# State sums in other banks, and four small copies on another engine, at a batch's first chunk

## The chip, the cores and the metric

The kernel runs on one core of a Trainium2 chip. The metric is the device time of one execution in microseconds (us), as the median of several runs. Five engines work side by side, each with its own queue of instructions: TensorE (PE in the profile, its weight loads PEld), VectorE (DVE), ScalarE (ACT), GpSimd (POOL) and SyncE (SP), which here only issues DMA transfers. An instruction at the head of a queue that has to wait holds up all that stand behind it on its engine. SBUF is the on-chip memory of 128 partitions; PSUM, in banks of 128 x 512 fp32 values, is where TensorE leaves its products.

## The reference

Two blocks follow each other. The first is a linear attention with decay, in blocks of 64 positions of a sequence of 768, for 4 batches and 8 heads of dimension 64:

```python
for b in range(nb):
    sl = slice(b * block, (b + 1) * block)
    qb, kb, vb = (q[:, :, sl], k[:, :, sl], v[:, :, sl])
    intra = np.einsum('bhic,bhjc->bhij', qb, kb) * Dmask[None]
    intra = np.einsum('bhij,bhjd->bhid', intra, vb)
    inter = np.einsum('bhid,bhde->bhie', qb * lam_pow[None], kv_state)
    out[:, :, sl] = intra + inter
    kb_dec = kb * rev_pow[None]
    kv_state = lam_block[None, :, None, None] * kv_state + np.einsum('bhsd,bhse->bhde', kb_dec, vb)
```

Its output x, as (batch, 768, 512), goes through a mixer: a low-rank product along the sequence that is added to x, and a product with 2048 hidden channels, a maximum with zero, and a product back:

```python
xt = x.transpose(0, 2, 1)
h = xt @ U @ V                       # U: 768 x 32, V: 32 x 768
u = x + h.transpose(0, 2, 1)
ch = np.maximum(u @ w_ch1, 0.0) @ w_ch2
return (u + ch).astype(np.float32)
```

## The kernel before, in words

The kernel treats the sequence in chunks of 128 positions, 6 to a batch, so 24 steps s; c = s mod 6 is the place in the batch and b the batch. A step works all 8 heads. One list, `pieces` (from line 646), written out by hand, gives the order in which the parts of the steps are issued; since each engine takes its instructions in the order of issue, this list sets every queue. The attention stage takes about the first 125 us of the span. Behind it come the two large products of the mixer (`hidden`, lines 830 and 841, and `product`, lines 962 to 966), which TensorE works almost without a gap.

A step's parts, by name and line:

- `prep` (line 361): TensorE turns q and k of the next chunk into two PSUM banks, tag pqk; ScalarE copies them out as qt and kt (line 367).
- `scores` (line 408): k times q into two banks, tag pss; `masked` (line 417): VectorE multiplies them by the decay mask and writes sm.
- `intra` (line 449): sm times v into px. `inter` (line 460): adds q times the state where c > 0; ScalarE then copies px out as x (line 466).
- `state` (line 427): k, scaled by GpSimd (ks, line 381), times v: the state's sums, in one bank. VectorE copies them to SBUF as kv where c = 0 (line 433) or adds the faded old state (line 435; faded is ScalarE's, line 401).
- `scale`: GpSimd's qs (line 392) and ks for the chunk after.
- `mix` (line 561) and `mixed` (line 573), of the chunk seven steps back: the low-rank correction, two matmuls with the high parts of the rows p_hl and two with the low parts, and VectorE's sum with x.
- `turn` (line 624), `split` (lines 638 and 639) and `turned` (line 631): the corrected x turned for the mixer and split into parts.

The rows of the low-rank product of a batch: `low` (line 476) sums them over the batch's six chunks in a bank. ScalarE (line 486) and VectorE (line 518) copy them to SBUF as rows_f, 32 partitions by 512; VectorE masks their high bits into t (line 521). Then `p_hl`, which is part of the tile vp, is filled in three parts that `low_rows` leaves in the list `pps[b]`, and that `next_of_low` takes out one at a time: `spread` copies quarters of t to four groups of 32 partitions (four copies of 32x256, line 529, ScalarE), `low_part` writes the differences rows_f - t into two groups (line 533, GpSimd), and `spread_low` copies these to the two other groups (line 540, ScalarE). The last batch goes another way (lines 496 to 511) that the change doesn't touch. The three parts are issued at the first chunk of the next batch, steps 6, 12 and 18.

The state's sums lie in the banks of tag pm up to step 6, and in those of the scores (pss) from step 7 on.

Of the kernel before, what the change touches and what calls it, by code (L numbers as in the profile page):

```python
# [18 lines left out]
def kernel(  # L19
# [28 lines left out]
    nc = tc.nc  # L48

    B, H, S, D = q.shape  # L50
    HP = H // 2
    NT = S // P
# [51 lines left out]
    def tmp(name):  # L104
        return wconv.tile([P, C], FP32, tag="tmp", bufs=2, name=name)
# [149 lines left out]
    def two_banks(name, tag):  # L255
        return psf.tile([P, 2, N], FP32, tag=tag, name=name)
# [162 lines left out]
    def state(s):  # L419
        c = s % NT  # L420
        if c < NT - 1:
            ks, vr = st[s]["ks"], raw[s, "v"]
            pkv = two_banks("pkv", "pm" if s <= NT else "pss")[:, 0, 0 : HP * D]
            pkv = pkv.rearrange("p (a e) -> p a e", a=HP)
            for a in range(HP):
                for x in range(2):
                    nc.tensor.matmul(  # L427
                        out=pkv[half[x], a, :], lhsT=ks[:, a, x, :], rhs=vr[:, 2 * a + x, :],
                        start=True, stop=True,
                    )  # L430
            kv[s + 1] = att.tile([P, HP, D], FP32, tag="kv", bufs=2, name="kv")
            if c == 0:
                nc.vector.tensor_copy(out=kv[s + 1], in_=pkv)  # L433
            else:
                nc.vector.tensor_tensor(out=kv[s + 1], in0=pkv, in1=st[s]["faded"], op=ALU.add)
# [33 lines left out]
    pps, others = {}, {}  # L469
# [19 lines left out]
    def low_rows(b):  # L489

        pp, t = pps.pop(b), tmp("p_h")[0:R]
        own = [(slice(g * R, (g + 1) * R), slice(g * P, (g + 1) * P)) for g in range(G)]
        if b == B - 1:
            h, h2, l, l2 = (p_hl[g * R : (g + 1) * R] for g in range(G))
            for rows, cols in own:
                nc.vector.tensor_scalar(
                    t[:, cols].bitcast(U32), pp[rows].bitcast(U32), HI, None, ALU.bitwise_and
                )

            def low_part():  # L500
                for rows, cols in own:
                    nc.vector.tensor_tensor(
                        out=l[:, cols], in0=pp[rows], in1=t[:, cols], op=ALU.subtract
                    )

            def spread():
                nc.scalar.copy(h, t)
                nc.scalar.copy(h2, t)

            def spread_low():  # L510
                nc.scalar.copy(l2, l.bitcast(FP32))

            pps[b] = [spread, low_part, spread_low]
            return

        rows_f, pp = pp, others.pop(b)
        for g in range(2, G):
            nc.vector.tensor_copy(
                out=rows_f[:, g * P : (g + 1) * P], in_=pp[g * R : (g + 1) * R]
            )  # L520
        nc.vector.tensor_scalar(t.bitcast(U32), rows_f.bitcast(U32), HI, None, ALU.bitwise_and)
        wide = [slice(x * 2 * P, (x + 1) * 2 * P) for x in range(2)]

        def place(g, low):
            return p_hl[g * R : (g + 1) * R, wide[low]]

        def spread():
            for g in range(G):
                nc.scalar.copy(place(g, 0), t[:, wide[g // 2]])

        def low_part():
            for x in range(2):
                nc.gpsimd.tensor_tensor(
                    out=place(2 * x, 1), in0=rows_f[:, wide[x]], in1=t[:, wide[x]],
                    op=ALU.subtract,
                )

        def spread_low():
            for x in range(2):
                nc.scalar.copy(place(2 * x + 1, 1), place(2 * x, 1).bitcast(FP32))  # L540

        pps[b] = [spread, low_part, spread_low]

    def next_of_low(b):
        pps[b].pop(0)()
# [102 lines left out]
    for s in range(NS):  # L648
        b, c = divmod(s, NT)
        done = s - NT - 1  # L650
        more = s + 1 < NS
        turns = done > 0 and (done - 1) // TG < FG
        mixes = 0 <= done < NS - NT - 1
        rows = c == 0 and b > 0
        step = [("fade", s)] * (c > 0)
        step += [("mix", done)] * mixes + [("turn", done - 1)] * turns
        step += [("split", done - 1)] * turns
        step += [("prep", s + 1)] * more
        step += [("mix", done + 1)] * (not more)
        step += [("next_of_low", b - 1)] * rows + [("next_of_low", b - 1)] * rows  # L660
        step += [("scale", s + 1)] * more
        step += [("mixed", done)] * mixes
        step += [("late", s - 1)] * (1 < s < NT - 1 or s > NT)
        step += [("turned", done - 2)] * (done > 1 and c == 1)
        step += [("mixed", done + 1)] * (not more)
        step += [("next_of_low", b - 1)] * rows
        both = [("intra", s), ("state", s)]
        step += (both if s > NT else both[::-1]) + [("next_v", s), ("inter", s)]
        step += [("late", s)] * (s < 2 or s in (NT - 1, NT))
        step += [("turned", done - 1)] * (done > 0 and c > 0)  # L670
        step += [("scores", s + 1)] * more
        step += [("low", b)] * (more and c == NT - 1)
        step += [("aside", s)] * (0 < s < NT - 2 or s > NT)
        step += [("masked", s + 1)] * more
        step += [("low_rows", b)] * (more and c == NT - 1)
        step += [("aside", s)] * (s in (0, NT - 2, NT - 1, NT))
        step += [("store", done)] * (done >= 0 and done // TG < FG)
        step += [("next_k", s)] * (s > 0)
        pieces += step
    waiting = {name: list(range(NS)) for name in "qkv"}  # L680

    def load_next(name, engine=nc.sync):
# [4 lines left out]
    run = {  # L687
        "prep": prep, "fade": fade, "scores": scores, "masked": masked, "inter": inter,
        "intra": intra, "state": state,
        "low": low, "low_rows": low_rows, "next_of_low": next_of_low, "mix": mix, "turn": turn,  # L690
        "mixed": mixed, "store": store, "next_v": next_v, "split": lambda s: splits.pop(s)(),
        
# [192 lines left out]
    c0, b = NS - NT, B - 1  # L885
# [129 lines left out]
    for i in range(len(steps) - STAG):  # L1015
        g, ft = steps[i]
# [49 lines left out]
```

## Time and profile before

| what | value |
|---|---|
| three runs | 652.66, 656.95, 657.25 us; median 656.95 |
| the profiled execution | 651.98 us, its span 650.1 us |
| granted TensorE clock | 1.000 |
| TensorE busy | 640.0 us, 98% of the span |
| VectorE, ScalarE, GpSimd busy | 441.4, 276.3, 116.6 us |
| the four copies of line 529 | 12 in all, 403 ns each, ScalarE |
| the differences of line 533 | 6 in all, 717 to 1023 ns, GpSimd |
| kv's copy, line 433 | 4 in all, 424 ns, VectorE |

The profile is of one execution. Times in a timeline count from the start of the span. In its lines stand the start, the busy time, the engine, the line of the kernel, the operation, output <- input by the program's names with partitions x elements, and how many of them were merged; in brackets the engine's idle time before, and what ended it. That releaser is inferred: where two ended nearly together, the other may be the one.

### The profile page before, as it was taken

What the parts mean: (1) busy time and instruction counts of PE and PEld (TensorE: products, weight loads), DVE (VectorE), ACT (ScalarE), POOL (GpSimd) and SP (SyncE); (2) the same over time, 40 slices, a digit from 0 to 9 for tenths busy, and PEclk for the clock granted to TensorE, in tenths of its full rate; (3) what the DMA queues carried; (4) which work ended last, traced back from release to release, by engine and by line L of the source; (5) the groups of instructions that cost most, each with busy time, mean ns of one, the idle gap of its engine ahead of it and who ended that gap; (6) DMA issues with size and microseconds to landing.
All of it is one profiled execution on the core that took longest, in us unless ns stands there. A gap on an engine that the chain in (4) does not pass through costs nothing.

```text
span 650.1 us, 13394 instructions
## 1 busy us (share of the span) xinstructions
PE 640.0 (98%) x5242; PEld 538.8 (83%) x5242; DVE 441.4 (68%) x710; ACT 276.3 (43%) x522; POOL 116.6 (18%) x98
## 2 busy tenths in 40 slices
PE   9999999999999999999999999999999999999997
PEld 8888988788888888888888888888888888888886
DVE  6779778658997777777796244685575665755854
ACT  4686876435664444444455221332332322322320
POOL 4476868240000000000000000030030300300300
PEclk9999999999999999999999999999999999999999
DMA  9999994264776656566687999864363363453521
GB/s 227 247 229 254 226 222 126 72 221 164 290 274 212 211 210 212 210 211 211 210 291 265 335 318 385 283 225 148 97 226 98 115 210 98 162 162 98 178 82 65
DMA packets 131776, 131.29 MB, mean 202 GB/s; under 512 B 81346, under 2 KB 89794, under 8 KB 131714
## 3 DMA queue, kind: packets, MB, share of 16 engines
q1 hardware_dynamic: 106592, 124.02, 59.2%
q10 hardware_dynamic: 25122, 6.42, 4.4%
q8 instruction: 41, 0.67, 0.4%
q14 instruction: 21, 0.17, 0.1%
HBM read 80.09 MB, written 50.33 MB: 201 GB/s over the span
## 4 chain that ended last, share of the span: by engine, by line
PE 92%; ACT 3%; DVE 2%; DMA 1%; issue 1%; ACTq 0%; DVEq 0%
PE pz L830 26%; PE pz L962 13%; PE pz L964 13%; PE pd L966 13%; PE pd L841 13%; PE pss L408 3%; PE px L449 3%; PE px L460 2%; PE pqk L361 1%; PE pkv L427 1%; PE pm L561 1%; DMA qraw<-in_q_dram 1%; PE pp L476 1%; DMA kraw<-in_k_dram 1%; PE pm L624 1%
## 5 line engine op out<-in xcount | busy, mean ns | idle before, releaser
L830 PE MATMUL pz<-u_hl,w 128*128 128x512 f32 x768 | 184.5, 390 | 0.0
L830 PEld LDWEIGHTS pz<-u_hl,w 128*128 128x128 f32 x768 | 143.7, 188 | 30.1 <-ACT r L837 0.3
L964 PE MATMUL pz<-w_hl,m 128*128 128x512 f32 x384 | 148.6, 389 | 0.0
L962 PE MATMUL pz<-w_hl,m 128*128 128x512 f32 x384 | 148.2, 389 | 0.0
L966 PE MATMUL pd<-w_d,m 128*128 128x512 f32 x384 | 147.4, 389 | 0.0
L945 ACT ACTIVATE m<-rm 128x512 fp32r<-128x512 f32 x96 | 60.6, 632 | 182.8 <-PE pd L966 125.1
L946 DVE SCALAR_TENSOR_TENSOR m<-rm,m 128x512 fp32r<-128x512 f32 x96 | 71.5, 747 | 95.9 <-ACT m L945 95.8
L991 POOL TENSOR_TENSOR o<-o,u 128x512 f32<-128x512 f32 x20 | 29.8, 1524 | 433.3 <-DVE o L987 433.3
L846 DVE SCALAR_TENSOR_TENSOR r<-pd,r 128x512 f32<-128x512 f32 x96 | 61.7, 684 | 60.3 <-ACT r L837 44.0
L841 PE MATMUL pd<-u_d,w 128*128 128x512 f32 x384 | 95.9, 390 | 0.0
L966 PEld LDWEIGHTS pd<-w_d,m 128*128 128x128 f32 x384 | 72.1, 188 | 15.2 <-DVE m L947 0.3
L964 PEld LDWEIGHTS pz<-w_hl,m 128*128 128x128 f32 x384 | 72.1, 188 | 15.0
L962 PEld LDWEIGHTS pz<-w_hl,m 128*128 128x128 f32 x384 | 72.1, 188 | 14.9
L841 PEld LDWEIGHTS pd<-u_d,w 128*128 128x128 f32 x384 | 71.9, 188 | 14.8
L837 ACT ACTIVATE r<-pz 128x512 f32<-128x512 f32 x96 | 51.8, 590 | 66.6 <-PE pz L830 66.5
L947 DVE SCALAR_TENSOR_TENSOR m<-m 128x512 fp32r<-128x512 f32 x96 | 74.7, 779 | 3.0
L417 DVE TENSOR_TENSOR sm<-pss,mask 128x512 f32<-128x512 f32 x48 | 30.9, 684 | 15.1 <-PE pss L408 14.9
L215 ACT ACTIVATE w<-wf 128x512 fp32r<-128x512 f32 x32 | 20.3, 634 | 34.8 <-DVE wf L197 27.0
L173 ACT ACTIVATE sc<-sc,ends 128x512 f32<-128x512 uint32 x30 | 21.6, 721 | 22.7 <-DVE sc L166 22.7
L408 PE MATMUL pss<-qt,kt 64*128 64x128 f32 x384 | 28.8, 290 | 2.4 <-DVE kv L433 1.2
L449 PE MATMUL px<-vraw,sm 128*64 128x64 f32 x768 | 28.0, 225 | 1.1 <-issue 0.5
L392 POOL TENSOR_TENSOR qs<-qt,powq 128x512 f32<-128x512 f32 x20 | 25.5, 1276 | 18.6 <-ACT qt L367 18.3
(91 smaller groups left out, 626.4 us busy)
## 6 DMA issues: line engine op xcount, KB each, us to landing
r_d<-r SPq DMA_DIRECT2D x96, 256.0 KB, 2.4
rm<-r_d SPq DMA_DIRECT2D x96, 256.0 KB, 2.7
words<-in_moe_w_ch_dram SPq DMA_DIRECT2D x30, 512.0 KB, 4.2
w_d<-w SPq DMA_DIRECT2D x16, 768.0 KB, 3.4
w_hl<-w_d SPq DMA_DIRECT2D x16, 512.0 KB, 6.0
u_d<-x_nat SPq DMA_DIRECT2D x24, 256.0 KB, 3.4
u<-u_d SPq DMA_DIRECT2D x24, 256.0 KB, 4.2
qraw<-in_q_dram SPq DMA_DIRECT2D x23, 256.0 KB, 3.7
```

Of the source, the lines that this page charges most:

```text
L408: nc.tensor.matmul(out=pss[:, x, a, :], lhsT=kt[half[x], a, :], rhs=qt[half[x], a, :], start=True, stop=True,)
L449: nc.tensor.matmul(out=px[half[t], x, a, :], lhsT=sm[:, x, a, half[t]], rhs=vr[:, 2 * a + x, :], start=(a == 0), stop=(alone and a == HP - 1),
L830: nc.tensor.matmul(out=like(acc[g][0], g), lhsT=w[:, n, ct, :], rhs=columns(uhl[g][:, n], g, ct), start=(ct == 0 and n == 0), stop=(ct == ...
L837: nc.scalar.mul(rs[g], acc[g][0], 4096.0 + 1.0)
L841: nc.tensor.matmul(out=like(acc[g][1], g), lhsT=w[:, 2, ct, :], rhs=columns(ud[g], g, ct), start=(ct == 0), stop=(ct == CT - 1),)
L846: nc.vector.scalar_tensor_tensor(rs[g], acc[g][1], 4096.0, rs[g], ALU.mult, ALU.add)
L945: nc.scalar.activation(out=m[:, 0], in_=r, func=AF.Relu, scale=NEAR)
L946: nc.vector.scalar_tensor_tensor(m[:, 1], r, 0.0, hi, ALU.max, ALU.subtract)
L947: nc.vector.scalar_tensor_tensor(m[:, 2], hi, E, low, ALU.mult, ALU.subtract)
L962: nc.tensor.matmul(out=pz, lhsT=m[:, 0, cols], rhs=hl[:, 0], start=first, stop=False)
L964: nc.tensor.matmul(out=pz, lhsT=m[:, 1, cols], rhs=hl[:, 1], start=False, stop=end)
L966: nc.tensor.matmul(out=pd, lhsT=m[:, 2, cols], rhs=dd, start=first, stop=end)
```

## The change

Three things change. At the first chunk of a batch (c = 0) from step 7 on, that is at steps 12 and 18, the state's sums go to the banks of tag pqk, in place of pss. The four copies of `spread` are issued to VectorE in place of ScalarE. And the three parts of the rows change order and place: `low_part` comes first, where `spread` and `low_part` stood; `spread` and `spread_low` come behind `inter`, that is behind kv's copy in VectorE's queue and behind x's copy in ScalarE's.

```diff
-            pkv = two_banks("pkv", "pm" if s <= NT else "pss")[:, 0, 0 : HP * D]
+            pkv = two_banks("pkv", "pm" if s <= NT else "pss" if c else "pqk")[:, 0, 0 : HP * D]
...
         def spread():
             for g in range(G):
-                nc.scalar.copy(place(g, 0), t[:, wide[g // 2]])
+                nc.vector.tensor_copy(out=place(g, 0), in_=t[:, wide[g // 2]])
...
-        pps[b] = [spread, low_part, spread_low]
+        pps[b] = [low_part, spread, spread_low]
...
         step += [("mix", done + 1)] * (not more)
-        step += [("next_of_low", b - 1)] * rows + [("next_of_low", b - 1)] * rows
+        step += [("next_of_low", b - 1)] * rows
         step += [("scale", s + 1)] * more
         step += [("mixed", done)] * mixes
         step += [("late", s - 1)] * (1 < s < NT - 1 or s > NT)
         step += [("turned", done - 2)] * (done > 1 and c == 1)
         step += [("mixed", done + 1)] * (not more)
-        step += [("next_of_low", b - 1)] * rows
         both = [("intra", s), ("state", s)]
         step += (both if s > NT else both[::-1]) + [("next_v", s), ("inter", s)]
+        step += [("next_of_low", b - 1), ("next_of_low", b - 1)] * rows
```

## The prediction

> **What bounds the kernel.** I read the page's first and fourth parts first: which engine fills the span, and which ends it.
>
> ```profile
> PE 640.0 (98%) x5242; PEld 538.8 (83%) x5242; DVE 441.4 (68%) x710; ACT 276.3 (43%) x522; POOL 116.6 (18%) x98
> ...
> PE 92%; ACT 3%; DVE 2%; DMA 1%; issue 1%; ACTq 0%; DVEq 0%
> ```
>
> TensorE is the bound: anything that leaves it idle in the attention stage (the first 125 us) moves the end. Two questions follow. Where does it have idle time around the change, and does anything later absorb a delay? The table of busy times by stretch answers both (columns: stretch, length, then busy us of each engine, granted clock, DMA share, GB/s).
>
> ```profile
> 63.00:70.00 7.00, 5.99 (x172) 5.57 (x171) 4.75 (x9) 6.58 (x17) 4.75 (x5) 1.00 0.82 199
> 73.00:88.00 15.00, 15.00 (x436) 14.07 (x432) 13.04 (x21) 11.03 (x26) 13.64 (x11) 1.00 1.08 243
> 125.00:400.00 275.00, 274.60 (x1223) 227.15 (x1222) 194.72 (x334) 124.20 (x214) 9.01 (x7) 1.00 0.69 243
> ```
>
> Around step 12 TensorE is busy 5.99 of 7.00 us and ScalarE 6.58 of 7.00. Between such places it is full (15.00 of 15.00), and behind the attention 274.60 of 275.00. So I count a delay at a changed step as reaching the end whole, once the step that follows has been worked through. Next comes the timeline of step 12, the first chunk of batch 2 (start, busy time, engine, line; step 18 repeats it 28.38 us later almost to the hundredth).
>
> ```profile
> 63.26 0.59 ACT L367 COPY kt<-pqk 128x512 f32<-128x512 f32 x1
> ...
> 63.40 1.51 POOL L533 TENSOR_TENSOR vp<-p_f,p_h 32x256 fp32r<-32x256 f32 x2 [3.72 <-ACT qt L367]
> 63.73 1.66 ACT L529 CAST vp<-p_h 32x256 fp32r<-32x256 f32 x4
> 63.77 0.58 PEld L427 LDWEIGHTS pkv<-vraw,ks 128*64 128x64 f32 x16
> ...
> 64.53 0.42 DVE L433 COPY kv<-pkv 128x256 f32<-128x256 f32 x1
> ...
> 64.99 1.26 POOL L392 TENSOR_TENSOR qs<-qt,powq 128x512 f32<-128x512 f32 x1
> ...
> 65.07 1.00 PEld L408 LDWEIGHTS pss<-qt,kt 64*128 64x128 f32 x16 [0.72 <-ACT vp L529]
> 65.10 1.13 PE L408 MATMUL pss<-qt,kt 64*128 64x128 f32 x15 [0.61 <-DVE kv L433]
> 65.42 0.83 ACT L540 CAST vp<-vp 32x256 fp32r<-32x256 f32 x2
> ...
> 66.21 1.06 POOL L381 TENSOR_TENSOR ks<-kraw,small 128x512 f32<-128x512 f32 x1
> ...
> 66.30 1.29 DVE L417 TENSOR_TENSOR sm<-pss,mask 128x512 f32<-128x512 f32 x2 [1.34 <-PE pss L408]
> ```
>
> The scores of step 13 (L408) wait 0.72 us because their banks hold the state's sums until VectorE has copied them (L433, end 64.95). That the weight loads name L529 is a tie in time: the scores read nothing of it. The next idle time is VectorE's 1.34 us before the mask (L417), which the change fills.
>
> **The change, part by part.**
>
> *State's sums in the banks of q and k (steps 12 and 18).* The scores no longer wait for L433. The new wait is that the sums need kt's copy to have left those banks: 63.26 + 0.59 = 63.85, and with 0.05 to TensorE 63.90 instead of 63.77, +0.13. Queued behind it is the whole TensorE queue. The loads without the wait would come at 65.07 - 0.72 = 64.35, so with the new wait at 64.48: 0.59 earlier, scores done 65.67. The banks are wanted again only by step 14's transposes, so the other side costs nothing. Step 6 keeps its banks.
>
> *Four copies leave ScalarE (L529, 4 x 0.40 = 1.61 us, three times).* x's copy (L466) is free about 1.6 us sooner, and the decay (L401) and the split (L638) behind it too. L540 now waits for x's copy but needs the GpSimd result (64.91) anyway; it ends about 66.0, earlier than before (66.25). Step 6: GpSimd ends 37.76, so L540 stays at 38.6. Queues: the v load that ScalarE issues is no longer behind L529; SP's issues keep their order; GpSimd's low parts keep their place before qs and ks.
>
> *Four copies arrive on VectorE, between the kv copy and the mask.* Work alone: nearest rows are L521, 32x512 within SBUF, 416 ns, and the 128x256 copy out of PSUM, 424 ns. L712 (64x384 within SBUF) takes 351, so 128 elements more cost 65 ns there, 0.51 ns each; out of PSUM 128 more cost 136 (L518's 288 at 128, L433's 424 at 256), 1.06 each. By the first, 256 elements take 416 - 256 x 0.51 = 285 ns, by the second 424. Bounds per copy: 0.28 and 0.42 us; 1.13 to 1.67 for four. I take 0.28, because L521 reads the same tile in the same memory.
>
> But they don't run alone: GpSimd runs qs and ks back to back there. What such an overlap does, another place in the trace shows (timeline of both engines, and the same line's larger shape elsewhere):
>
> ```profile
> 13.53 1.28 POOL L392 TENSOR_TENSOR qs<-qt,powq 128x512 f32<-128x512 f32 x1 [1.54 <-ACT qt L367]
> 14.77 1.07 POOL L381 TENSOR_TENSOR ks<-kraw,small 128x512 f32<-128x512 f32 x1
> ```
> ```profile
> 13.85 1.08 DVE L166 TENSOR_SCALAR sc<-words 128x192 uint32<-128x192 uint32 x1
> 14.85 1.11 DVE L155 TENSOR_SCALAR m<-words 128x192 uint32<-128x192 uint32 x1
> ```
> ```profile
> L166 DVE TENSOR_SCALAR sc<-words 128x512 uint32<-128x512 uint32 x2 | 0.8, 419 | 0.0
> ```
>
> 192 elements take 1080 ns, 512 elsewhere 419. L166 ends 0.12 after qs (14.81), L155 0.12 after ks (15.84): each VectorE instruction waits a whole GpSimd instruction out, and they alternate. Instructions that read PSUM aren't held (the masks of L417 at 99.81 take 1.29 us, as everywhere, beside GpSimd's L381 and L631). No copy within SBUF of this size is in the trace, so its cost lies between no hold and this one. I take the hold: L166 too has one SBUF input and SBUF output.
>
> The Trainium skill says the same more widely: "SBUF — State Buffer", section "Who interferes with whom", lists copy and cast with `tensor_scalar` among what can take the port pair shared with GpSimd, exclusively, whoever starts first. By it the sum is my likeliest case; were it wrong for this copy, the third case below. It speaks against this change, which trades a wait on banks for one on a port; no run here yet shows it for a copy.
>
> *Step 12 with the hold.* kv copy after the sums, 64.66 to 65.08; qs began 64.99, so copy 1 ends 66.25 + 0.15 = 66.40. ks goes next: copy 2 ends near 67.5. GpSimd is then empty (its next is at 68.98), copies 3 and 4 end 67.75 and 68.0. The correction's matmuls (L561) need all four: the turn (L624, before at 66.30) starts at 68.3. The mask runs 68.0 to 69.3. The intra product (L449, before 67.35, 1.05 after the turn) starts 69.35, +2.0, its second mask half just in time. State(13) ends 68.97 + 2.0 = 70.97, kv's sum 71.0 to 71.4, scores(14) 71.5 instead of 70.19: **+1.3**. The 0.7 recovered is time in which VectorE, held up behind ScalarE's split (0.87 idle), was late with kv's sum before. The same at step 18.
>
> *Step 6 with the hold.* The kv copy ends 37.62 as before, L533's second half holds copy 1 until 37.91, qs copy 2 until 39.3, ks copy 3 until 40.35; copy 4 ends 40.6. The transposes of prep start 40.9 instead of 38.71, intra(7) 41.7 instead of 39.52, its inter product ends 43.8, scores(8) start 43.85 instead of 41.79: **+2.05**.
>
> *Sum:* 2.05 + 2 x 1.3 = +4.65 us. The profiled execution took 651.98, so its like would be 656.6. The runs shown are 652.66, 656.95 and 657.25: the median lies 4.97 above the profile, as much as the change is worth. I put the sum on the median, since that is what is compared: 656.95 + 4.65 = **661.6**, +0.7%.
>
> **Rivals.**
>
> *Copies at full length, unheld* (0.42), or *held once and then through together*. Full length: step 12's copies end 66.75, intra(13) 68.1, scores(14) 70.25, +0.06; step 6's end 39.3, scores(8) 42.5, +0.7; sum +0.8. Held once: step 12 ends 67.15, +0.4 each; step 6 about +0.15; sum +0.95. Both about +0.9: 657.9. For: the copy changes type and partitions, as L166 doesn't. Against: the strict alternation at 13.85.
>
> *Faster: the freed banks win.* Copies of 0.28, unheld: they end 66.2, within VectorE's old idle time; the turn starts 66.5 (+0.2), intra(13) 67.55, kv's sum 69.6, scores(14) 69.75 instead of 70.19: -0.45, twice; step 6 +0.25. Sum -0.65: 656.3. It decides from where the four copies end before about 66.9, when scores(14) come even. For: a wait of 0.72 really goes, and ScalarE is relieved by 1.6 us. Against: the rows of L166 and L155.
>
> *It doesn't do what it says:* the wait of 0.72 is ScalarE's L529, as the load's releaser has it, not the banks. The copies leave ScalarE anyway, so the wait goes in this case too; only another owner of the time is named, and the sum stays.
>
> **Numbers.** Hold with alternation 0.65; the two at +0.9 together 0.2; faster 0.1; something unseen, mostly slower, 0.05. The four executions of before spread over 5.3 us, so a measurement can tell about 1% (6.6 us) from no change. All cases have centres inside it; the likeliest can cross it if a hold is longer or the median falls badly (about 1 in 6): slower 0.13, faster 0.03, same 0.84. Its own range is +3 to +6, 660 to 663 on the median, 655 to 658 on the profile. The whole range reaches from a low execution with +1.5 (653.5) to the median with +8 (665).
>
> **What would show it.** Right: the four VectorE copies (32x256) at steps 12 and 18 last over 1 us for the first two and under 0.35 for the last; L408's wait behind L433 gone; a new TensorE idle time of about 2 us before L561's second half; the mask 1.7 us later. At step 6 three copies drawn out. Wrong: all copies of 0.28 or 0.42; ks drawn out instead of the copies (VectorE keeps the port); a step behind with TensorE idle that takes the delay in, against the 15.00 of 15.00 above.

## The result and the profile after

The changed kernel takes 661.78 us (median of seven runs, 660.81 to 663.17). The kernel before, in seven runs, takes 652.66 (651.14 to 657.25). The ratio is 1.0121, with a 95% interval of 1.0085 to 1.0157: slower by about 8 us. The profiled executions are 9.5 us apart in their spans, 659.6 against 650.1. One execution among those below, of the last version, ran at a granted clock of 0.56 throughout and took 1060.33 us; it is left out of every ratio.

The predicted time of 661.6 us is met almost exactly, but by luck: two errors cancel. The change costs 8 to 9.5 us and not 4.65, which is also outside the prediction's own range for it, +3 to +6. And the median of the three runs shown before the prediction, 656.95, was high: of those three two lay near 657, of the four taken later one reached 656.04 and the others lie between 651.14 and 652.05. The mechanism that the prediction names is there; a second one, which it doesn't price, doubles the loss.

The page of the changed kernel, first the busy times, then the granted clock in 40 slices of 16.5 us, then the chain that ended last:

```profile
PE 644.9 (98%) x5242; PEld 543.6 (82%) x5242; DVE 448.4 (68%) x722; ACT 272.4 (41%) x510; POOL 116.7 (18%) x98
...
PEclk9989898999999999999999999999999999999999
...
PE 94%; DVE 3%; DMA 1%; ACT 1%; issue 1%; ACTq 0%; DVEq 0%
```

VectorE is busy 7.0 us longer: the twelve copies have joined it, 8.5 us by their row, 0.71 each, two and a half times the 0.28 forecast for one alone. TensorE, which does the same work, is busy 4.9 us longer. The clock shows why: three slices stand at 8 tenths, and all were at 9 (90% or more) before. They hold steps 7, 13 and 19, the steps right behind the three changed places.

The timeline of step 12 in the changed kernel answers to the one shown of before (start, busy time, engine, line):

```profile
68.79 0.97 PEld L408 LDWEIGHTS pss<-qt,kt 64*128 64x128 f32 x16
...
68.85 1.27 POOL L392 TENSOR_TENSOR qs<-qt,powq 128x512 f32<-128x512 f32 x1
...
68.90 0.42 DVE L433 COPY kv<-pkv 128x256 f32<-128x256 f32 x1 [0.50 <-PE pkv L427]
69.24 2.71 DVE L529 CAST vp<-p_h 32x256 fp32r<-32x256 f32 x4
...
70.08 1.10 POOL L381 TENSOR_TENSOR ks<-kraw,small 128x512 f32<-128x512 f32 x1
...
71.39 0.38 PE L561 MATMUL pm<-vp 64*128 64x256 f32 x1 [1.43 <-DVE vp L529]
71.98 1.29 DVE L417 TENSOR_TENSOR sm<-pss,mask 128x512 f32<-128x512 f32 x2
...
72.00 0.50 PE L561 MATMUL pm<-vp 64*128 64x256 f32 x3 [0.24 <-DVE vp L529]
...
73.57 1.97 PE L449 MATMUL px<-vraw,sm 128*64 128x64 f32 x32
```

The scores (L408) no longer wait: their loads follow the state's at once. The four copies take 2.71 us together. TensorE then waits 1.43 and 0.24 us for them. The last line is what no step of the prediction has: the intra product takes 1.97 us, and 1.15 in the kernel before.

The chain of waits in the same stretch takes the copies apart (start, length, what):

```profile
69.33 0.94 DVE vp L529
...
70.28 1.05 DVE vp L529
...
71.36 0.28 DVE vp L529
...
71.66 0.30 DVE vp L529
```

The first copy ends 0.15 us after qs (68.85 + 1.27 = 70.12), the second 0.15 after ks (71.18), and the last two, with GpSimd empty, take 0.28 and 0.30. This is the alternation that the prediction read from L166 and L155.

The table of stretches shows the clock (the third number from the end) there:

```profile
70.00:71.00 1.00, 0.00 (x0) 0.00 (x0) 0.99 (x2) 0.94 (x3) 1.00 (x2) 1.00 0.89 193
72.50:73.00 0.50, 0.50 (x18) 0.50 (x14) 0.50 (x2) 0.18 (x1) 0.00 (x0) 0.59 0.20 45
73.00:73.50 0.50, 0.50 (x11) 0.45 (x8) 0.32 (x2) 0.41 (x1) 0.00 (x0) 0.50 0.08 18
...
75.50:76.00 0.50, 0.50 (x16) 0.50 (x14) 0.00 (x0) 0.00 (x0) 0.17 (x1) 0.50 1.03 289
76.00:76.50 0.50, 0.50 (x26) 0.43 (x26) 0.17 (x1) 0.00 (x0) 0.13 (x1) 1.00 0.86 250
```

TensorE is busy 0.00 of the microsecond from 70 to 71. From about 72.6 to 76.0, some 3.4 us, its clock is at half. By the time the copies are done the wait is over, but the work behind it runs at half speed.

### The profile page after: what moved, and what is told of

Same layout as the page of the kernel before. It is cut to its first block, busy times and chain, and to the rows that moved or that the text cites. A ratio compares the mean times of both kernels' runs of the same rounds, so it can differ in the third digit from the quotient of the medians.

```text
span 659.6 us, 13395 instructions
## 1 busy us (share of the span) xinstructions
PE 644.9 (98%) x5242; PEld 543.6 (82%) x5242; DVE 448.4 (68%) x722; ACT 272.4 (41%) x510; POOL 116.7 (18%) x98
## 4 chain that ended last, share of the span: by engine, by line
PE 94%; DVE 3%; DMA 1%; ACT 1%; issue 1%; ACTq 0%; DVEq 0%
PE pz L830 26%; PE pz L964 13%; PE pz L962 13%; PE pd L966 13%; PE pd L841 13%; PE px L449 4%; PE pss L408 3%; PE pqk L361 2%; PE px L460 2%; PE pkv L427 2%; DVE vp L529 1%; PE pp L476 1%; PE pm L561 1%; DMA qraw<-in_q_dram 1%; PE pm L624 1%
## 5 line engine op out<-in xcount | busy, mean ns | idle before, releaser
L449 PE MATMUL px<-vraw,sm 128*64 128x64 f32 x768 | 31.3, 239 | 1.3 <-issue 0.8
L449 PEld LDWEIGHTS px<-vraw,sm 128*64 128x64 f32 x768 | 28.2, 151 | 3.2 <-issue 1.5
```

Source lines behind the costliest of these rows:

```text
L449: nc.tensor.matmul(out=px[half[t], x, a, :], lhsT=sm[:, x, a, half[t]], rhs=vr[:, 2 * a + x, :], start=(a == 0), stop=(alone and a == HP - 1),
```

## The experiments

A measure of one place. TensorE's time from the batch's low-rank sums (the start of L476 in the last step of a batch) to the scores two steps later (the start of L408) encloses one changed place. In the kernel before it is 9.55 us around step 6 and 10.24 around steps 12 and 18. In the changed kernel it is 12.89, 13.05 and 13.02: +3.34, +2.81 and +2.78, 8.93 of the 9.5 us by which the spans differ; another 0.50 lies ahead of the first place, where L476 starts at 32.78 instead of 32.28. Between the places nothing is taken in: from scores(8) to the next L476 it is 18.16 us before and 18.18 after.

Two theories. **A:** the copies wait out GpSimd's instructions, TensorE goes idle, and that idle time brings the clock down. **B:** the clock falls for another reason (the copies, the port, the kernel as a whole).

### Filling TensorE's wait

```diff
+            spare = two_banks("idle", "pqk")[:, 0, 0:P] if c == 0 else None
+            fill = [(7, 4), (6, 1), (6, 1)][b]
             for low in range(2):
                 for x in range(2):
+                    for i in range(fill[x] if c == 0 and low == 0 else 0):
+                        nc.tensor.matmul(
+                            out=spare, lhsT=ident, rhs=ident, start=True, stop=True
+                        )
                     nc.tensor.matmul(
                         out=pm[:, x], lhsT=weights[half[x]],
```

> The changed kernel, with idle-filling matmuls (128x128, into a spare bank, results unused) issued on TensorE where it waits for the copies: 7 before and 4 behind the correction's first matmul at step 7, 6 and 1 at steps 13 and 19. Theory A (the copies' hold idles TensorE, and the idle time brings its clock to half for 3.4 us): the copies stay drawn out, the granted clock stays 1.00 at all three places, L449 there takes 1.15 us instead of 1.97, and of the 9.5 us about half goes: some 657 beside 652 for the kernel before, ratio 1.007 to 1.009. Rival B (the clock falls for a reason other than TensorE's idle time): the clock still falls to 0.50, and the time stays at 661 to 662. Rival C (the matmuls themselves get in the way): above 662.

Measured: 657.6 us (656.66 to 659.15), ratio 1.0074 (1.0048 to 1.0101). The copies are as long as before, the clock stays up. The copies by their line, then the timeline of steps 12 and 13:

```profile
L529 DVE CAST vp<-p_h x12: 281/660/1394, 37.7 to 100.1; 32x256 fp32r<-32x256 f32 x12
```
```profile
68.09 1.60 PE L564 MATMUL idle<-ident 128*128 128x128 f32 x12
...
69.96 0.38 PE L567 MATMUL pm<-vp 64*128 64x256 f32 x1 [0.26 <-DVE vp L529]
...
71.86 1.15 PE L449 MATMUL px<-vraw,sm 128*64 128x64 f32 x32
```

Useless work in the wait makes the kernel 4 us faster: L449 is back at 1.15 us. The places now cost +2.42, +1.43 and +1.42. Theory B and rival C fall: the copies are as long, and only TensorE's idle time has gone.

### The same with fewer matmuls

The edit is the list alone: `[(4, 2), (3, 0), (3, 0)]`, then `[(2, 1), (1, 0), (1, 0)]`.

> As the fill experiment, with about half the idle-filling matmuls (4 and 2 at step 7, 3 and 0 at steps 13 and 19; two passes of each take about 0.27 us). About 1.3 us of TensorE's idle time is left at each place, in two parts. Theory A (the clock falls by the idle time around it): this is close to the 1.4 to 1.6 us that cost the clock with the copies on ScalarE, and far above the 0.6 us that did not before, so it falls at some places at most: between 657 (none) and 661 (all). If it falls nowhere the bound lies above 1.3 us, if everywhere below it.

> As the fill experiment, with few of the idle-filling matmuls (2 and 1 at step 7, 1 and 0 at steps 13 and 19). About 1.8 to 2.0 us of idle time is left at each place. Theory A: the clock falls to 0.50 at all three, time 660 to 662 as without any. Rival B (it is the presence of some work, not the sum of idle time, that keeps the clock): it stays at 1.00, 657.

Measured: with half, 657.28 us (655.88 to 660.23), ratio 1.0064 (1.0041 to 1.0086), clock 1.00 at all three places of the profile. The places cost +2.03, +1.32 and +1.31, together 4.66. With a sixth, 660.67 us (657.44 to 663.35), ratio 1.0111 (1.0075 to 1.0146). Its profile shows the clock at 0.50 behind step 18 only. From the timelines, what was left of TensorE's wait, with half and then with a sixth of the matmuls, at steps 13 and 19:

```profile
71.65 0.38 PE L567 MATMUL pm<-vp 64*128 64x256 f32 x1 [0.76 <-DVE vp L529]
72.26 0.50 PE L567 MATMUL pm<-vp 64*128 64x256 f32 x3 [0.24 <-DVE vp L529]
```
```profile
71.81 0.38 PE L567 MATMUL pm<-vp 64*128 64x256 f32 x1 [1.11 <-DVE vp L529]
...
100.61 0.38 PE L567 MATMUL pm<-vp 64*128 64x256 f32 x1 [0.47 <-DVE vp L529]
101.98 0.50 PE L567 MATMUL pm<-vp 64*128 64x256 f32 x3 [0.98 <-DVE vp L529]
```

Waits of 0.76 + 0.24 us keep the clock. 0.47 + 0.98 lose it, though 1.11 + 0.23 at step 13 and 1.22 + 0.59 at step 7 of the same execution keep it. So the expectation that a sixth loses it everywhere was wrong, and no single sum of idle time decides.

Where the waits lie does much of it. In every trace the clock's changes lie whole multiples of 3.41 us apart: in the changed kernel it falls at 41.87, 72.59 and 103.31, nine such steps from one to the next, and is back 3.41 later each time. With a sixth it falls at 102.77. Counted back from there in the same steps, these are the stretches that hold the waits (the first two numbers behind the stretch are its length and TensorE's busy time):

```profile
37.92:41.33 3.41, 2.19 (x28) 1.72 (x23) 3.30 (x5) 2.46 (x7) 3.26 (x4) 1.00 0.99 237
41.33:44.74 3.41, 2.81 (x70) 2.58 (x69) 2.81 (x5) 1.07 (x2) 1.09 (x2) 1.00 0.12 29
68.64:72.05 3.41, 2.30 (x38) 1.86 (x33) 2.96 (x5) 2.28 (x7) 2.89 (x3) 1.00 0.94 222
99.36:102.77 3.41, 1.96 (x32) 1.45 (x30) 3.33 (x5) 2.22 (x8) 2.12 (x2) 1.00 1.06 233
```

The 1.22 + 0.59 us are split between two stretches, and the 0.47 + 0.98 lie in one, which is idle for 1.45 us and ends where the clock falls. In the changed kernel the stretches that end at its falls are idle for 2.33, 1.67 and 2.03 us. The bound isn't sharp: a stretch with 1.49 us of idle time keeps the clock in the run with three copies further down.

The spread of this kernel's runs, 5.9 us, goes with the falls. One fall to half for 3.41 us lowers the mean clock of a run by about 0.0026. The three shorter runs (657.44 to 659.55 us) have 0.995 to 0.997, the three longer ones (661.78 to 663.35) 0.990 to 0.992, as much as the changed kernel's 0.988 to 0.992.

### GpSimd's work behind the copies

```diff
+    def behind(s):
+        last = p_hl[(G - 1) * R : G * R, 0:2].bitcast(FP32)
+        nc.gpsimd.tensor_tensor(
+            out=small[(G - 1) * R : G * R, 1:3], in0=last, in1=last, op=ALU.subtract
+        )
...
-        step += [("scale", s + 1)] * more
+        step += [("scale", s + 1)] * (more and not rows)
...
+        step += [("behind", s), ("scale", s + 1)] * rows
```

> The changed kernel, with GpSimd's qs and ks of these three steps put behind the copies: one tiny GpSimd instruction that reads what the last copy wrote comes ahead of them. Theory A (each copy waits out a whole GpSimd instruction): all copies take about 0.28 us, the four end near 1.1 us after kv's copy, L561's wait falls under 0.3 us, the clock stays 1.00, and the time comes to that of before, between -0.9 and +0.5 us. Rival D (the copies are long by themselves, by the change of type or of partitions): they stay between 0.4 and 1.4 us and the time stays above 656. At step 6 the first copy still meets the second half of the low parts and is long.

Measured: 651.96 us (651.16 to 653.37), ratio 0.9989 (0.9976 to 1.0002), clock 1.00. The copies by their line, and the first ones behind kv's copy at step 12:

```profile
L529 DVE CAST vp<-p_h x12: 272/284/288, 37.8 to 94.6; 32x256 fp32r<-32x256 f32 x12
```
```profile
65.57 1.20 DVE L529 CAST vp<-p_h 32x256 fp32r<-32x256 f32 x4
...
66.83 0.71 PE L567 MATMUL pm<-vp 64*128 64x256 f32 x3 [0.25 <-DVE vp L529]
```

The same copies on the same engine at the same place take 284 ns once GpSimd does nothing beside them, and the whole loss is gone. TensorE's wait for the fourth copy is down to 0.25 us. Rival D falls: neither the change of type nor that of partitions makes them long. The places are at +0.26, -0.31 and -0.30, near the price of the prediction's third case ("Faster: the freed banks win": +0.25, -0.45, -0.45). One detail of the expectation is wrong: the first copy of step 6 wasn't made long by the low parts, none of the twelve was over 288 ns.

### The banks alone

The edit is the first line of the change's diff, in the kernel before.

> The kernel before with the banks alone changed: state's sums of steps 12 and 18 in the banks of q and k; copies on ScalarE in their old place. Theory A (the wait removed is followed by the next one): the scores start 0.6 us sooner, but L561 still waits for L540's end at the old time, so the turn L624 starts where it did; 0 to -0.3 us in all. Rival E (the wait of the scores was on the path by itself): -0.6 at each of two steps, -1.2 us. Either way within what the measurement can tell, so the timeline decides.

Measured: 651.89 us, ratio 0.9986 (0.9968 to 1.0003). The places of steps 12 and 18 measure 10.25 and 10.25, against 10.24. The timeline shows where the wait went:

```profile
65.06 0.97 PEld L408 LDWEIGHTS pss<-qt,kt 64*128 64x128 f32 x16
...
66.37 0.18 PEld L561 LDWEIGHTS pm<-vp 64*128 64x128 f32 x1 [0.23 <-ACT vp L540]
...
66.80 0.18 PEld L561 LDWEIGHTS pm<-vp 64*128 64x128 f32 x1 [0.24 <-ACT vp L540]
...
70.70 1.00 PEld L408 LDWEIGHTS pss<-qt,kt 64*128 64x128 f32 x16 [0.75 <-ACT kt L367]
```

The scores don't wait, but the correction's matmuls wait for L540. Counted from L476, the turn starts where it did (6.32 us in both kernels), and scores(14) too: theory A, and rival E (-0.6 at each) falls.

### The new order with the copies on ScalarE

```diff
-                nc.vector.tensor_copy(out=place(g, 0), in_=t[:, wide[g // 2]])
+                nc.scalar.copy(place(g, 0), t[:, wide[g // 2]])
```

> The changed kernel with the four copies back on ScalarE, but in the new place and order (behind x's copy), and with the new banks. Theory A: no hold (0.40 each), but they queue behind x's copy and ahead of L540, which then ends about 1.4 us later than before at steps 12 and 18 and 1.0 at step 6. Without loss of clock +0.9 us at each place, +2.8 in all, about 655; if the idle time, broken up into parts of 0.4 to 0.8 us, also takes the clock, up to +2.5 at each, about 659. Rival F (the port alone makes the loss): the time of before, 652.

Measured: 660.33 us (658.95 to 661.17), ratio 1.0107 (1.0076 to 1.0138). The clock falls behind all three places, which cost +3.77, +2.40 and +2.67. At step 12:

```profile
70.31 1.66 ACT L529 CAST vp<-p_h 32x256 fp32r<-32x256 f32 x4
...
71.18 0.38 PE L561 MATMUL pm<-vp 64*128 64x256 f32 x1 [0.73 <-ACT vp L529]
...
72.03 1.23 PE L561 MATMUL pm<-vp 64*128 64x256 f32 x3 [0.46 <-ACT vp L529]
...
73.93 1.56 PE L449 MATMUL px<-vraw,sm 128*64 128x64 f32 x32
```

Nothing is held here (1.66 = 4 x 0.41), and the loss is nearly the same. So the port isn't the only way to lose: the new place, behind x's copy, is late for ScalarE's unheld 1.66 us too. Rival F falls. The clock fell here after less idle time than elsewhere: the stretches of 3.41 us that end at its falls show 1.39, 0.68 and 0.99 us of it. So idle time as the profile counts it isn't the whole rule; what makes the difference here wasn't tested.

### Steps 12 and 18 alone

The change without its part at step 6, whose copies stay on ScalarE in the old order.

> The change at steps 12 and 18 alone; step 6 as in the kernel before (copies on ScalarE, old place and order). Theory A (the three places add up): of the 9.5 us that the profiles of before and after are apart, the 3.6 to 3.9 of step 6 go and 2 x 2.8 stay: +5.6, some 658. Rival H (a delay at one place is taken in by the later ones): under +4 or over +7.

Measured: 657.93 us (656.14 to 659.99), ratio 1.0068 (1.0039 to 1.0097), so about +4.4, with a wide interval around the +5.6 expected. In its profile the places of steps 12 and 18 cost +2.71 and +3.73. The places add up, as far as runs that differ by 4 us can say.

### Idle time without copies or port

The kernel before, with kv's copy out of PSUM made three or five times at steps 12 and 18:

```diff
-                nc.vector.tensor_copy(out=kv[s + 1], in_=pkv)
+                for i in range(3 if s > NT else 1):
+                    nc.vector.tensor_copy(out=kv[s + 1], in_=pkv)
```

> The kernel before, with kv's copy out of PSUM made three times at steps 12 and 18 (the same values each time): no copy within SBUF, no port, only some 0.8 us more of TensorE's unbroken wait before the scores, about 1.4 us by its own row instead of 0.61. Theory A (idle time alone brings the clock down): it may or may not fall at this size. Without a fall +0.1 us at each, 653; with one +1.6 at each, 656.

> The same with five copies: the wait is about 2.2 us. Theory A: the clock falls to 0.50 for about 3.4 us at both places; +0.9 us by the delay and +1.5 by the clock at each, some 657.5. Rival B (the clock falls for the copies or the port, not for idle time): it stays at 1.00, some 654.5.

Measured: 655.55 us, ratio 1.0037 (1.0008 to 1.0067), and 658.09 us, ratio 1.0059 (1.0033 to 1.0085). The scores of step 13 with three copies, then with five:

```profile
68.21 1.13 PE L408 MATMUL pss<-qt,kt 64*128 64x128 f32 x15 [1.52 <-DVE kv L434]
```
```profile
71.21 1.55 PE L408 MATMUL pss<-qt,kt 64*128 64x128 f32 x16 [2.44 <-ACT x_nat L467]
```

And the stretches behind the wait with five:

```profile
72.00:74.00 2.00, 2.00 (x33) 2.00 (x32) 1.21 (x2) 0.57 (x2) 0.00 (x0) 0.50 0.58 131
74.00:76.00 2.00, 2.00 (x51) 1.88 (x49) 1.37 (x3) 1.32 (x3) 0.78 (x1) 0.69 0.33 77
```

The releaser that the second row names is a near tie: the fifth copy ends at 71.07. After 1.52 us the clock stays at 1.00 in the profile, after 2.44 it falls at both places. Idle time is enough, with no copy within SBUF on VectorE near it. The same profile shows a third fall, at 27.46, where the edit changes nothing: TensorE had just been idle for 1.69 us without a break. And a wait of 2.44 us doesn't always cost the clock: of this kernel's ten runs one (656.45 us) has a mean clock of 1.000, so no fall at all.

With three copies the time isn't explained. Without a fall 653 was expected; nine of the ten runs have a mean clock of 0.999 or more, and the median is 655.55. In the profile the places cost +0.10 and +1.51, the second with a wait of 1.24 us inside L461 that the profile puts down to no releaser.

### A version that beats both

GpSimd's work behind the copies at steps 12 and 18, step 6 as before, and ScalarE's issue of v's load behind the low parts. This is the part that is new, against the kernel of "GpSimd's work behind the copies"; the lines that put step 6 back aren't shown:

```diff
-        step += (both if s > NT else both[::-1]) + [("next_v", s), ("inter", s)]
-        step += [("next_of_low", b - 1), ("next_of_low", b - 1)] * rows
-        step += [("behind", s), ("scale", s + 1)] * rows
+        new = rows and s > NT
+        step += (both if s > NT else both[::-1]) + [("next_v", s)] * (not new) + [("inter", s)]
+        step += [("next_of_low", b - 1), ("next_of_low", b - 1)] * new
+        step += [("behind", s), ("scale", s + 1), ("next_v", s)] * new
```

> A version meant to win: GpSimd's qs and ks behind the copies as in the experiment with that order, at steps 12 and 18 alone, step 6 as before, and ScalarE's issue of v's load behind the low parts, so that x's copy and L540 come sooner. Theory A: the state's wait of 0.6 us is gone, the copies are not held, L540 ends ahead of the fourth copy; 0.3 to 0.6 us gained at each of two steps, -0.6 to -1.2 us in all (ratio 0.998 to 0.999). Rival: the next wait takes it, no difference.

> The version of the experiment before once more, for its profile: ratio 0.997 to 0.999; the four copies 0.28 us each, the scores directly behind the state's sums, L540 ended before the correction's fourth matmul wants it, the clock 1.00.

Measured: 651.41 us, ratio 0.9969 (0.9946 to 0.9993), then 651.31 us (650.21 to 652.95), ratio 0.9951 (0.993 to 0.9973). Step 12 in the second:

```profile
65.83 0.97 PEld L408 LDWEIGHTS pss<-qt,kt 64*128 64x128 f32 x16
...
66.28 1.18 DVE L532 CAST vp<-p_h 32x256 fp32r<-32x256 f32 x4
...
66.37 0.40 ACT L543 CAST vp<-vp 32x256 fp32r<-32x256 f32 x1
...
67.52 0.50 PE L570 MATMUL pm<-vp 64*128 64x256 f32 x3 [0.23 <-DVE vp L532]
...
70.89 1.00 PEld L408 LDWEIGHTS pss<-qt,kt 64*128 64x128 f32 x16
```

No wait before the scores, copies unheld, the low parts (L543) done before the fourth copy. The two places measure 9.66 and 9.71, -0.58 and -0.53: -1.1 us, and 0.4 of it shows in the spans (649.7 against 650.1); the way to the first place took 1.3 us more in this execution. The ratios say 2 to 3 us. The rest isn't explained: the runs of before beside the two reach up to 659.9 and 659.6, those counted of this version stay below 653.3.

## Why the prediction was right and wrong

- **The bank's wait goes, the wait for kt is small.** Right. With the banks alone the state's loads start 0.15 us later and the scores' 0.50 sooner (counted from L476; 0.13 and 0.59 were forecast), and that gains nothing by itself because the correction's matmuls have the next wait.
- **ScalarE is relieved.** Partly wrong, though it decided nothing here. x's copy was to come about 1.6 us sooner and L540 to end earlier. Counted from L476, x's copy (L466) starts 0.72 us sooner at step 12, and L540 ends 0.74 later: ScalarE's issue of v's load stands ahead of them and waits, ScalarE being idle for 1.69 us before x's copy. With that issue behind L540, in the last version, step 12 comes to -0.58 instead of -0.31.
- **The copies take 0.28 us each.** Right: 284 ns at the median, unheld.
- **The hold.** Right, to hundredths at step 12: copy 1 ends 0.15 us after qs, copy 2 after ks, the last two free. The strict alternation read from L166 and L155 holds for a copy. At step 6 two copies are drawn out (1.29 and 1.03 us) and not three: the first meets only the last 0.1 us of L533 and takes 0.28.
- **+1.3 us at steps 12 and 18, +2.05 at step 6, 4.65 in all.** Right for what was counted: with the clock kept up by half the fill, the places cost 1.32, 1.31 and 2.03, 4.66 in all (with the full fill 1.43, 1.42 and 2.42).
- **The term that was missing** stands in the sentence "The intra product (L449, before 67.35, 1.05 after the turn) starts 69.35, +2.0" and what follows it: every instruction behind the wait was given its old duration. TensorE's idle time of 1.7 to 2.9 us brought its clock to 0.50 for some 3.4 us. That cost 12.89 - 11.58 = 1.31 us at step 6, 13.05 - 11.56 = 1.49 at step 12 and 13.02 - 11.55 = 1.47 at step 18: 4.3 us, nearly as much as the wait itself. The prediction said that TensorE would be idle for about 2 us, showed the clock column, and didn't put the two together.
- **The chances.** "Same", within about 1%, had 0.84 and "slower" 0.13; the ratio is 1.0121, with an interval that reaches down to 1.0085. The chances came from a sum that lacked the clock, so they were too sure.
- **The base.** Putting the sum on the median of three, 656.95, and not on the profiled 651.98, hid the missing term. The changed kernel's own runs lie within 2.4 us.
- **The rivals.** Copies at full length and copies held once: neither occurs. The faster case is what the kernel does when GpSimd's work is out of the way.

The Trainium skill has the clock in "TensorE: Matmul & The Clock Gate", Part 1: half rate is the default, it comes back after at least one idle window of about 3.4 us, and the window runs freely. The low stretch measured here, 72.6 to 76.0, agrees with that length. The freely running window agrees with the steps of 3.41 us at which the clock changes in the traces. The condition doesn't agree if the window has to be idle throughout: stretches with 1.45 to 2.44 us of idle time out of 3.41 were followed by half rate.

## What to carry to other kernels

Before moving copies within SBUF from ScalarE to VectorE, look at what GpSimd runs at that moment: here a copy of 0.28 us took 1.0 to 1.4 beside it, and one instruction that orders GpSimd behind the copies gave all of it back. When an edit adds a wait to a TensorE that is otherwise full, price the wait twice: by its length and by the 1.3 to 1.5 us that the slower clock behind it cost here. In these runs the second price has to be feared once TensorE's waits within 3.4 us add up to about 1.2 us or more (0.73 + 0.46 lost the clock, 1.52 kept it), and it then depends on where they fall. And when a profile and a median of few runs disagree by as much as the effect, predict the difference, not the time.

## What the runs showed of the hardware

- TensorE's clock fell to 0.50 for 3.41 us (6.83 in two cases) after idle times of 1.43 + 0.24, 0.47 + 0.98, 0.73 + 0.46, 1.69 and 2.44 us; it stayed after 0.76 + 0.24, 1.11 + 0.23, 1.22 + 0.59 and 1.52. Its changes lie multiples of 3.41 us apart within an execution, and where the idle time lies in these steps matters. Useless matmuls in the gap kept it up and saved 4 us of 661.78.
- Within SBUF, VectorE's copy waits out whole instructions of GpSimd's arithmetic, and the two engines take turns: the copies took 0.94 and 1.05 us of the chain beside qs and ks, 0.28 and 0.30 behind them. At GpSimd's side the cost is small (ks took 1.10 us, otherwise 1.06), at VectorE's side it is the whole of the other instruction.
